# q's low part on 128 partitions, the softmax guard on GpSimd, v without its zero blocks, and new leads for the planner

## The chip, the core and the metric

The kernel runs on one core of a Trainium2 chip. Its engines work side by side, each through its own queue in order: TensorE (PE, with its weight loads shown apart as PEld), VectorE (DVE), ScalarE (ACT), GpSimd (POOL), and SyncE (SP), which issues the DMAs. The metric is the device time of one execution in microseconds; of several runs the median counts.

## The reference, cut to what matters

```python
def reference(q, k, v, f, moe_w_in, moe_w_out, moe2_w_in, moe2_w_out, moe2_alpha):
    # q, k, v: (4, 8, 576, 64) float32, f: (4, 8, 576)
    cum = np.cumsum(np.log(np.clip(f, 0.0001, 1.0)), axis=-1)
    scores = q @ k^T / sqrt(64) + cum[..., :, None] - cum[..., None, :]   # causal: -1e9 above the diagonal
    attn = np.exp(scores - max(scores))
    attn = attn / (np.sum(attn, axis=-1, keepdims=True) + 1e-09)
    x = (attn @ v) as (2304, 512)
    h = x @ moe_w_in;  x = np.maximum(0.01 * h, h) @ moe_w_out            # 512 -> 2048 -> 512
    h = x @ moe2_w_in; g = np.maximum(h, 0) + moe2_alpha * np.minimum(h, 0)
    return g @ moe2_w_out
```

So there are a causal attention with a forgetting decay for 32 heads, and two feed-forward layers (here MoE1 and MoE2) over 2304 tokens.

## The kernel before, in words

**Numbers in two parts.** TensorE multiplies float32r tiles faster than float32 ones, but with fewer bits. So nearly every operand is split in a high part (a cast to float32r) and a low part (the operand minus its high part), and a product becomes three. `cast` (L404 on ScalarE, L406 on VectorE) makes high parts and `sub` (L409) low parts. The expert weights come raw, are taken apart (L487 to L507), split, and partly parked in DRAM scratch (`wscr`), from where they come back as `ws` (L573).

**Stages.** Four batches and two parts of the sequence (queries 0 to 320 and 320 to 576) make 8 groups of 8 heads. The first two groups (some 60 us) use plain float32 and load q, k and v as they are (*native*). The other six groups, 48 heads, use the split form and are laid between MoE1's matmuls (L604 is h, L650 is y), up to about 480 us. MoE1 goes on to 608 us. MoE2 runs from there to the end, with seven products per block (L761) in place of eight, and its second matrix (L830).

**One split head.** SP loads `qk` (L922): 128 partitions, where the upper 64 hold the head's q and k and the lower 64 hold them again. `qk_hi` casts all of it to `k1`. `q_lo` replaces the lower 64 partitions of q's columns with q minus its high part, so that one matmul of 128 rows gives two of the three products. `k_lo` writes k's low part to `k2`. The row of the decay's cumulative sum is broadcast into `cb` by DMA (L929), and GpSimd masks it (`dm`, L1097; for the first heads `cb`, L1104). v arrives in `vr` for two heads at once (L914): the host array has three blocks of 64 columns, the first head's v, zeros and the second head's v; `v_hi` and `v_lo` read the first and the third of them. The scores (L1131) get the decay and the mask on VectorE (L1145), then ScalarE's exp (L1156), which also sums the row into `nm`. A `guard` adds 1e-9 to the sum (L1001) and `recip` inverts it (L1004), both on VectorE, for two rows of blocks at a time. Then the weights are normalised (L1171 on ScalarE, L1173 on VectorE or GpSimd), transposed on TensorE (L1186), split as `pt` (L1202) and multiplied with v (L1034; native L1024). The output is shifted and added into `xr` (L1075, L1078) and split as `xp`.

**What sets the order.** No engine's order is written by hand. `Plan.op` records each operation with its time on each engine that may do it and with a due time; `Plan.run` simulates the engines and lets each take, of the operations that are ready, the one due first. An operation counts as ready when what it reads has ended, plus a latency for the pair of engines (`latency`, L120). Where several engines may do it, the cheapest takes it: VectorE's `shared` operations and GpSimd's exclude each other in the simulation, with `PRICE` on top. The instructions are then issued in the simulated order. The due times come from a row of constants: `PROL`, `PROL0` and `FIRST0` set the first stage, `AHEAD` how early weights are loaded, `W2LEAD`, `W2FROM`, `W2EACH`, `W2STEP` and `W2OUT` when MoE2's weights are made ready, `LEAD1`, `LASTSPAN`, `LASTH` and `ATTN` the pace of the heads, `PACKLEAD` and `DMALAT` the loads.

```python
        return (0 if a == "pe" else 125) if a == b else 260 if b == "pe" else 200 if a == "pe" else 170
```

Of the kernel before, what the change touches and what calls it, by code (L numbers as in the profile page):

```python
# [18 lines left out]

P = 128  # L20
EXCL = 1
WT = {"dve": 1.0, "act": 1.0, "pool": 1.0}
OLD = 0
SUBD = 1
RECIPS = 2
MARGIN = 450
AHEAD = 7600
NRAW = 4
CW = 512
NCV = 3  # L30
NAT = 16
PACKLEAD = 5200
ORDER = (0, 0, 0, 0, 1, 1, 1, 1)
NSTREAM = 18
NSTR = 4
# [8 lines left out]
NGR = 2  # L44
NG = 3
NYSB = 2
W2LEAD = 112200
NEARLY = 4
W2FROM = 2.77
W2EACH = 0.68  # L50
W2LAG = 51000
W2STEP = 5300
W2OUT = 8400
AHEAD2 = 16300
NR = 8
NG2 = 5
# [1 line left out]
NWARM = 5  # L58
PAIRS = (0, 3, 5, 7)
SHIFT = 1  # L60
PROL = 52000
PROL0 = 26000
FIRST0 = 99000
FREE = 8
ATTN = 12800
LASTH = 10600
W1LEAD = 12500
LEAD1 = 24000
LEAD2 = 54900
DMALAT = 2600  # L70
BATCH = 1
LASTSPAN = 1.04
STEP = 4
PRICE = 0.25
MASKED = 2.0**30


# [33 lines left out]
class Plan:  # L111
# [8 lines left out]
    @staticmethod  # L120
    def latency(a, b):

        if "dma" in (a, b):
            return DMALAT * (a == "dma") + 1250 * (b == "dma")
        return (0 if a == "pe" else 125) if a == b else 260 if b == "pe" else 200 if a == "pe" else 170

    def op(self, times, due, fn, r=(), w=(), a=(), after=(), hold=(), shared=False, busy=1.0):

# [148 lines left out]
def t_act(n):  # L277
    return 0.833 * n + 90
# [14 lines left out]
def t_pool1(n):  # L293
    return 0.833 * n + 245
# [19 lines left out]
def tile_forgetting_attention_two_moe(ctx: ExitStack, tc, qk0, qk1, v0, v1, fg, w1, w2, alphaT, out):  # L314
# [126 lines left out]
    rings["g"].ordered = False  # L441
    ring("ysb", NYSB, [P, 2, T])
    ring("qk", 2, [P, 256 + S], pool="att")
    ring("vr", 2, [P, 5, 3, D], pool="att")
    ring("cb", 3, [P, S], pool="att")
    ring("k1", 1, [P, 256 + S], F32R, pool="att")
    ring("k2", 1, [P, S], F32R, pool="att")
# [11 lines left out]
    ring("pt0", 2, [P, 1408], pool="att0")  # L459
    ring("tri", 1, [P, 2 * P], F32R)  # L460

    rate = const.tile([B * H, 2], F32, name="rate")
    warm = const.tile([1, 1], F32, name="warm")
    yd = dram.tile([P, NC, NT], F32, name="yd")
    wscr = dram.tile([NF, 2, P, 2, 512], F32, name="wscr")
    w2in = dram.tile([NP, 4, P, 2, 512], F32, name="w2in")
    cum_d = dram.tile([B * H, 2, S], F32, name="cum_d")

    warm_b, cum_b, yd_b, wscr_b, w2_b, rate_b = (Buf(Ring(1, None)) for _ in range(6))
    for b, ap in ((warm_b, warm), (cum_b, cum_d), (yd_b, yd), (wscr_b, wscr), (w2_b, w2in), (rate_b, rate)):  # L470
        b.ap = ap
    tri_b = new("tri")

# [7 lines left out]
    def assemble(which, f, half, d, after=()):  # L481

        raw, v = new("raw"), new("cv")
        src = (w1, w2)[which].bitcast(I32)[f, :, 2 * CW * half : 2 * CW * (half + 1)]

        def load():
            sp.dma_start(out=raw.ap, in_=src.rearrange("p (n t) -> p n t", t=2))  # L487

        def rebase(e):
            high = f32(raw.ap[:, :, 1])  # L490
            if e == "act":
                act.activation(out=f32(v.ap), in_=high, func=AF.Copy, scale=2.0**-112)
# [12 lines left out]

        def low():
            dve.scalar_tensor_tensor(  # L507
                out=v.ap, in0=raw.ap[:, :, 0], scalar=29, in1=v.ap, op0=ALU.logical_shift_right, op1=ALU.bitwise_or
            )

        on("dma", t_dma(8 * CW * P), EARLY if (which, f) == (0, 0) else d - 5e3, load, w=[raw], after=after)
        plan.op({"act": t_act(CW), "pool": t_pool1(CW)}, d, rebase, r=[raw], w=[v])
        on("dve", t_dve2(CW), d, bits, w=[v], shared=True)
        on("dve", t_dve(CW), d, sign, r=[raw], w=[v], shared=True)
        on("dve", t_dve(CW), d, low, r=[raw], w=[v], shared=True)
        return v
# [353 lines left out]
    def attention_heads(gi, hs, d, span):  # L870
# [29 lines left out]
        for e, h in enumerate(hs):  # L900
# [10 lines left out]
            hi, lo = (0, D) if even else (D, 0)  # L911
            if even:
                vr = x_raw["v"] = new("vr0" if native else "vr")
                on("dma", t_dma(3 * nkt * D * 4 * P), dh - (6e3 if native else 12e3), lambda: sp.dma_start(  # L914
                    out=vr.ap[:, :nkt], in_=g["v"][b, h // 2]), w=[vr])

            apart = not native or gi == 0 and h < 2
            width = n + keys if apart else 2 * (n + keys)
# [12 lines left out]
            def qk_hi(en, k1=k1, qk=qk):  # L931
                cast(en, k1.ap[:, : n + keys], qk.ap[:, : n + keys])

            def q_lo(en, k1=k1, qk=qk):
                sub(en, k1.ap[D:P, :n], qk.ap[D:P, :n], f32(k1.ap[D:P, :n]))

            def k_lo(en, k1=k1, k2=k2, qk=qk):
                sub(en, k2.ap[:, :keys], qk.ap[:, n : n + keys], f32(k1.ap[:, n : n + keys]))

            def v_hi(en, v2=v2, h=h, hi=hi, o2=o2):  # L940
                cast(en, v2.ap[:, o2 : o2 + nkt, hi : hi + D], vr.ap[:, :nkt, h % 2 * 2, :])

            def v_lo(en, v2=v2, h=h, hi=hi, lo=lo, o2=o2):
                sub(en, v2.ap[:, o2 : o2 + nkt, lo : lo + D], vr.ap[:, :nkt, h % 2 * 2, :], f32(v2.ap[:, o2 : o2 + nkt, hi : hi + D]))

            m = full[-1][0] + P
            if apart or e == 0:
# [31 lines left out]
                        lambda: pair.ap[half, both : both + keys], r, keys), r=[(cum_b, g["i"])], w=[(pair, 1 + e)])  # L979
            if not native:  # L980
                plan.op(t_cast(n + keys), dh - 2e3, qk_hi, r=[qk], w=[k1], shared=True)
                plan.op(t_sub(n), dh - 2e3, q_lo, r=[qk], w=[(k1, "q")], shared=True)
                plan.op(t_sub(keys), dh - 2e3, k_lo, r=[qk, (k1, "k")], w=[k2], shared=True)
                plan.op(t_cast(nkt * D), dh + each, v_hi, r=[vr], w=[(v2, (e, "hi"))], shared=True)
                plan.op(t_sub(nkt * D), dh + each, v_lo, r=[vr, (v2, (e, "hi"))], w=[(v2, (e, "lo"))], shared=True)
# [10 lines left out]
        for i, u, t, es, du in todo:  # L996
            if i % RECIPS == 0:
                i1 = min(i + RECIPS, len(todo))

                def guard(i=i, i1=i1):  # L1000
                    dve.tensor_scalar(out=nm.ap[:, 3, i:i1], in0=nm.ap[:, 2, i:i1], scalar1=1e-9, scalar2=None, op0=ALU.add)  # L1001

                def recip(i=i, i1=i1):
                    dve.reciprocal(out=nm.ap[:, 3, i:i1], in_=nm.ap[:, 3, i:i1])  # L1004

                both = [(nm, k) for k in range(i, i1)]
                on("dve", 70, du, guard, w=both)
# [5 lines left out]
    def attention_out(g, t0, h, e, dd, vr, v2, o2, lo, hi, pt, pt_ap, native):  # L1013
# [65 lines left out]
                out=xr.ap[hi : hi + D, :n], in0=po.ap[hi : hi + D, :n], in1=xr.ap[hi : hi + D, :n], op=ALU.add  # L1079
            )  # L1080

        on("act", t_act(n) - 40, dd, shift, r=[po], w=[(xr, h % 2)])
        on("dve", t_dve(n), dd, add, r=[po], w=[(xr, h % 2)])
        if not even:
            split(xr, False)

# [331 lines left out]
```

## Time and profile before

| | us |
|---|---|
| three runs | 992.1, 993.36, 994.47 |
| median | 993.36 |
| profiled execution | 991.83 |
| its span, first to last instruction | 989.7 |

| engine | busy us | share | instructions |
|---|---|---|---|
| TensorE | 976.0 | 99% | 5170 |
| TensorE weight loads | 842.6 | 85% | 5170 |
| VectorE | 746.7 | 75% | 1849 |
| ScalarE | 536.2 | 54% | 1231 |
| GpSimd | 90.1 | 9% | 161 |

Line numbers (L1001) are those of the kernel before. A row names the tiles as out<-in without buffer numbers. Busy time of TensorE counts matmuls with a modelled end, so short gaps vanish in it; the weight loads show them. "<-ACT t L1171" names what ended an idle time: here a tile t written by ScalarE in line 1171. A share over the whole span is a mean over stages that differ.

### The profile page before, as it was taken

How to read it: one execution, taken by the hardware profiler on the slowest of the kernel's cores; microseconds unless marked ns; L12 is line 12 of the kernel's file. 1: busy time of each engine (PE TensorE's matmuls, PEld its weight loads, DVE VectorE, ACT ScalarE, POOL GpSimd, SP SyncE). 2: the span in 40 equal slices, each digit the busy share in tenths (PEclk: the TensorE clock that was granted, in tenths of full speed). 3: DMA queues.
4: the chain of work that ended last, by engine and by line, in shares of the span. 5: the costliest groups of instructions: out<-in, count | busy, mean ns of one | idle time of the engine just before them, and what ended most of it. 6: DMA issues, size and time to landing. Idle time of an engine off the chain costs nothing.

```text
span 989.7 us, 15662 instructions
## 1 busy us (share of the span) xinstructions
PE 976.0 (99%) x5170; PEld 842.6 (85%) x5170; DVE 746.7 (75%) x1849; ACT 536.2 (54%) x1231; POOL 90.1 (9%) x161
## 2 busy tenths in 40 slices
PE   9999999999999999999999999999999999999998
PEld 7777777999888878878878888889889898988987
DVE  7798999887998897986776647856696656856563
ACT  8987887996887777867646435211232112321112
POOL 2101233211211120211000000000000000000000
PEclk9999999999999999999999999999999999999999
DMA  8869887688767789845497765533374333634311
GB/s 285 286 202 320 284 316 229 207 297 285 259 228 267 242 275 320 271 145 174 138 368 253 262 213 173 175 111 118 107 245 129 127 118 107 203 121 144 105 46 64
DMA packets 76128, 203.27 MB, mean 205 GB/s; under 512 B 8112, under 2 KB 23248, under 8 KB 76048
## 3 DMA queue, kind: packets, MB, share of 16 engines
q1 hardware_dynamic: 76048, 202.28, 61.2%
q8 instruction: 41, 0.67, 0.3%
q14 instruction: 39, 0.32, 0.1%
HBM read 168.57 MB, written 33.67 MB: 204 GB/s over the span
## 4 chain that ended last, share of the span: by engine, by line
PE 76%; DVE 10%; issue 6%; DMA 4%; ACT 4%; POOL 1%; POOLq 0%; ACTq 0%; SPq 0%; DVEq 0%
PE bank L830 20%; PE bank L761 18%; PE bank L650 12%; PE bank L604 12%; PE bank L1131 5%; PE bank L1186 3%; PE bank L1034 3%; DMA raw<-w 2%; PE bank L1024 1%; DVE pt L1202 1%; DVE k L409 1%; DVE t L1145 1%; DMA w2in<-wa 1%; DVE cv L507 1%; DVE g L409 1%
## 5 line engine op out<-in xcount | busy, mean ns | idle before, releaser
L830 PE MATMUL bank<-w,g 128*128 128x512 f32 x756 | 196.9, 393 | 0.0
L404 ACT ACTIVATE g<-r 128x384 fp32r<-128x384 f32 x96 | 50.4, 526 | 256.3 <-DVE r L793 232.5
L770 DVE TENSOR_TENSOR r<-bank,r 128x384 f32<-128x384 f32 x168 | 91.0, 555 | 91.1 <-PE bank L761 90.9
L830 PEld LDWEIGHTS bank<-w,g 128*128 128x128 f32 x756 | 140.1, 188 | 21.2
L650 PE MATMUL bank<-g,ws 128*128 128x512 f32 (+1 forms) x540 | 128.0, 374 | 1.3 <-ACT g L404 1.3
L604 PE MATMUL bank<-xp,ws 128*128 128x512 f32 (+1 forms) x540 | 126.3, 372 | 0.0
L650 PEld LDWEIGHTS bank<-g,ws 128*128 128x128 f32 x540 | 92.1, 189 | 18.2 <-ACT g L404 3.7
L604 PEld LDWEIGHTS bank<-xp,ws 128*128 128x128 f32 x540 | 93.3, 189 | 15.2
L650 PE MATMUL bank<-g,w 128*128 128x512 f32 (+1 forms) x420 | 101.4, 375 | 0.1
L604 PE MATMUL bank<-xp,w 128*128 128x512 f32 (+1 forms) x420 | 99.2, 374 | 0.1
L1156 ACT ACTIVATE t<-t,nm 128x128 f32<-128x128 f32 (+4 forms) x144 | 83.9, 586 | 24.6 <-DVE nm L1145 24.2
L604 PEld LDWEIGHTS bank<-xp,w 128*128 128x128 f32 x420 | 72.1, 189 | 12.4 <-ACT t L1171 0.5
L650 PEld LDWEIGHTS bank<-g,w 128*128 128x128 f32 x420 | 71.8, 189 | 12.1 <-ACT g L404 0.7
L1202 DVE TENSOR_TENSOR pt<-bank,pt 128x128 fp32r<-128x128 f32 (+2 forms) x136 | 64.1, 504 | 22.2 <-ACT pt L404 21.7
L1097 POOL TENSOR_SCALAR_AFFINE_SELECT dm<-cb 128x448 f32<-128x448 f32 (+1 forms) x96 | 54.9, 573 | 264.1 <-DVE nm L1145 224.2
L1171 ACT ACTIVATE t<-t,nm 128x128 f32<-128x128 f32 (+4 forms) x112 | 58.8, 564 | 28.7 <-DVE nm L1004 27.5
L409 DVE TENSOR_TENSOR g<-r,g 128x384 fp32r<-128x384 f32 x96 | 53.2, 554 | 25.9 <-ACT g L404 25.9
L404 ACT ACTIVATE pt<-bank 128x512 fp32r<-128x512 f32 (+6 forms) x176 | 67.6, 433 | 4.3 <-PE bank L1186 3.6
L1186 PE MATMUL bank<-tri,t 128*128 128x128 f32 x432 | 65.8, 277 | 1.7 <-DVE t L1173 0.5
L409 DVE TENSOR_TENSOR g<-gr,g 128x512 fp32r<-128x512 f32 x72 | 50.4, 700 | 18.4 <-ACT g L404 18.3
L1186 PEld LDWEIGHTS bank<-tri,t 128*128 128x128 f32 x432 | 49.3, 141 | 15.0 <-ACT t L1171 5.3
L1034 PEld LDWEIGHTS bank<-pt,v 128*128 128x128 f32 x416 | 55.8, 189 | 5.9 <-ACT pt L404 1.9
(136 smaller groups left out, 1687.0 us busy)
## 6 DMA issues: line engine op xcount, KB each, us to landing
ws<-wscr SPq DMA_DIRECT2D x72, 512.0 KB, 4.9
raw<-w SPq DMA_DIRECT2D x64, 512.0 KB, 5.8
wa<-w2in SPq DMA_DIRECT2D x33, 512.0 KB, 3.5
ws<-w2in SPq DMA_DIRECT2D x33, 512.0 KB, 3.5
qk<-qk SPq DMA_DIRECT2D x32, 416.0 KB, 4.7
wscr<-ws SPq DMA_DIRECT2D x18, 512.0 KB, 5.6
cb<-cum_d SPq DMA_DIRECT2D x32, 288.0 KB, 4.4
vr<-v SPq DMA_DIRECT2D x16, 480.0 KB, 5.1
```

The lines of the kernel that those rows point to most:

```text
L404: act.activation(out=out, in_=in_, func=AF.Copy)
L409: (dve if e == "dve" else gps).tensor_tensor(out=out, in0=in0, in1=in1, op=ALU.subtract)
L604: pe.matmul(h()[:, i] if single else h(), lhsT=w.ap[:, a, c * P : (c + 1) * P], rhs=xs[0].ap[:, s, c] if single else xp[:, x0 : x0 + 2, s, c],
L650: pe.matmul(out(c), lhsT=w.ap[:, a, col : col + P], rhs=g.ap[:, s, at : at + n], start=f == 0 and (a, s) == (0, 0) and (c % 2 == 0 or not ...
L761: pe.matmul(b.ap[:, :N2], lhsT=t.ap[:, a, o + c * P : o + (c + 1) * P], rhs=view(k)[:, s, c], start=c == 0 and i == 0, stop=c == 1 and i == 2,
L770: on("dve", t_dve(N2), d + k * step - URGENT, lambda: dve.tensor_tensor(out=out.ap, in0=b.ap[:, :N2], in1=x.ap, op=ALU.add), r=[b] if x is ...
L830: pe.matmul(acc[j * (N2 // P) + t].ap, lhsT=g.ap[:, s, t * P : (t + 1) * P], rhs=w.ap[:, a], start=p == 0 and i == j and (a, s) == (0, 0), ...
L1034: pe.matmul(po.ap[:, q:n], lhsT=v2.ap[:, o2 + j, :], rhs=pt_ap(s, e, j, j + 1, q, n), start=s == 0 and j == 0, stop=s == 1 and j == nkt - 1,)
L1156: act.activation(out=t.ap[:, :nk], in_=t.ap[:, :nk], func=AF.Exp, scale=-1.0, bias=nm.ap[:, last, u : u + 1], accum_out=nm.ap[:, 2, u : u ...
L1171: act.activation(out=t.ap[:, :nk], in_=t.ap[:, :nk], func=AF.Copy, scale=nm.ap[:, 3, u : u + 1])
L1186: pe.transpose(tp.ap[:, (j - j0) * P : (j - j0 + 1) * P], t.ap[:, k0 : k0 + P], f32(tri_b.ap[:, :P]))
L1202: dve.tensor_tensor(out=lo, in0=src, in1=f32(hi), op=ALU.subtract)
```

## The change

Four things change. `q_lo` is no longer a subtraction on 64 partitions by VectorE or GpSimd, but one scalar_tensor_tensor on all 128 by VectorE alone: high part times a column `lower` plus q, where the column is 0 for the upper 64 partitions and −1 for the lower (a new tile `rates` holds it beside the old `rate`). The guard's addition goes to GpSimd, the reciprocal stays on VectorE. Split heads load only the two blocks of v that are read, so that each partition's row becomes pieces of 256 bytes; native heads load as before. And the planner's latencies, times and due times are set anew; latencies have names now. Lines shift by 5 (around L490 to L930) and then by 7.

```diff
+TOSAME = 125
+TOPE = 315
+FROMPE = 200
+CROSS = 200
-AHEAD = 7600
+AHEAD = 5100
-PACKLEAD = 5200
+PACKLEAD = 6100
...
-PROL = 52000
-PROL0 = 26000
-FIRST0 = 99000
+PROL = 53600
+PROL0 = 24200
+FIRST0 = 94700
...
-DMALAT = 2600
+DMALAT = 3200
...
-        return (0 if a == "pe" else 125) if a == b else 260 if b == "pe" else 200 if a == "pe" else 170
+        return (0 if a == "pe" else TOSAME) if a == b else TOPE if b == "pe" else FROMPE if a == "pe" else CROSS
...
-    ring("vr", 2, [P, 5, 3, D], pool="att")
+    ring("vr", 2, [P, 5, 2, D], pool="att")
...
-    rate = const.tile([B * H, 2], F32, name="rate")
+    rates = const.tile([P, 3], F32, name="rates")
+    rate, lower = rates[: B * H, :2], rates[:, 2:]
...
-        plan.op({"act": t_act(CW), "pool": t_pool1(CW)}, d, rebase, r=[raw], w=[v])
+        plan.op({"act": t_act(CW) + 50, "pool": t_pool1(CW)}, d, rebase, r=[raw], w=[v])
...
-                on("dma", t_dma(3 * nkt * D * 4 * P), dh - (6e3 if native else 12e3), lambda: sp.dma_start(
-                    out=vr.ap[:, :nkt], in_=g["v"][b, h // 2]), w=[vr])
+                on("dma", t_dma((2 + native) * nkt * D * 4 * P), dh - (6e3 if native else 12e3), lambda: sp.dma_start(
+                    out=vr.ap[:, :nkt], in_=g["v"][b, h // 2] if native else g["v"][b, h // 2][:, :, ::2]), w=[vr])
...
-            def q_lo(en, k1=k1, qk=qk):
-                sub(en, k1.ap[D:P, :n], qk.ap[D:P, :n], f32(k1.ap[D:P, :n]))
+            def q_lo(k1=k1, qk=qk):
+                dve.scalar_tensor_tensor(
+                    out=k1.ap[:, :n], in0=f32(k1.ap[:, :n]), scalar=lower, in1=qk.ap[:, :n], op0=ALU.mult, op1=ALU.add
+                )
...
-                plan.op(t_sub(n), dh - 2e3, q_lo, r=[qk], w=[(k1, "q")], shared=True)
+                on("dve", t_dve(n), dh - 2e3, q_lo, r=[qk, lower_b], w=[(k1, "q")], shared=True)
...
-                    dve.tensor_scalar(out=nm.ap[:, 3, i:i1], in0=nm.ap[:, 2, i:i1], scalar1=1e-9, scalar2=None, op0=ALU.add)
+                    gps.tensor_scalar(out=nm.ap[:, 3, i:i1], in0=nm.ap[:, 2, i:i1], scalar1=1e-9, scalar2=None, op0=ALU.add)
...
-                on("dve", 70, du, guard, w=both)
+                on("pool", 180, du, guard, w=both)
...
-        on("act", t_act(n) - 40, dd, shift, r=[po], w=[(xr, h % 2)])
-        on("dve", t_dve(n), dd, add, r=[po], w=[(xr, h % 2)])
+        on("act", t_act(n) + 90, dd, shift, r=[po], w=[(xr, h % 2)])
+        on("dve", t_dve(n) + 100, dd, add, r=[po], w=[(xr, h % 2)])
...
+    for i in range(2):
+        on("pool", 100, -9.4e3, lambda i=i: gps.memset(lower[i * D : i * D + D], -1.0 * i), a=[(lower_b, i)])
```

The rest of the constants: W2LEAD 112200 to 114600, W2FROM 2.77 to 2.753, W2EACH 0.68 to 0.762, W2STEP 5300 to 4900, W2OUT 8400 to 9300, ATTN 12800 to 12200, LASTH 10600 to 13600, LEAD1 24000 to 24800, LASTSPAN 1.04 to 1.083, PRICE 0.25 to 0.141.

Three places show how the order moves. The first is VectorE's queue at 608 us, where MoE1 ends. `bx`, `xp`, `xt` and `yraw` belong to MoE2's input, `w` is one of its weights, `ws` a weight from scratch. Before:

```order
L409 TENSOR_TENSOR ws_7168<-cv_6369,ws_7168 128x256
L406 CAST w_7184<-cv_7112 128x512
L409 TENSOR_TENSOR w_7184<-cv_7112,w_7184 128x512
L409 TENSOR_TENSOR bx_6254<-yraw_7153,bx_6254 128x384
L409 TENSOR_TENSOR xp<-yraw_7153,xp 128x384
L409 TENSOR_TENSOR bx_6307<-yraw_7153,bx_6307 128x384
```

Now:

```order
L413 TENSOR_TENSOR ws_7169<-cv_6381,ws_7169 128x256
L413 TENSOR_TENSOR bx_6292<-yraw_7123,bx_6292 128x384
L413 TENSOR_TENSOR xp<-yraw_7123,xp 128x384
L413 TENSOR_TENSOR bx_6347<-yraw_7123,bx_6347 128x384
...
L413 TENSOR_TENSOR bx_6336<-xt_7200,bx_6336 128x384
L413 TENSOR_TENSOR xp<-yraw_7123,xp 128x384 x2
L413 TENSOR_TENSOR w_7224<-cv_7141,w_7224 128x512
```

The cast of `w` has left VectorE's queue for ScalarE's, and its low part has moved behind all of the splits of MoE2's first input.

The second is GpSimd's queue in the first stage: `cb` masks (L1104, now L1111), rebased weights `cv` (L494, now L499), and guards (`nm`, L1008). Before:

```order
L1104 TENSOR_TENSOR cb_0_145<-cb_0_145,tri_115 64x64 x2
L1104 TENSOR_TENSOR cb_1_163<-cb_1_163,tri_115 64x64 x2
L494 TENSOR_SCALAR cv_241<-raw_182 128x512
L494 TENSOR_SCALAR cv_267<-raw_202 128x512
L1104 TENSOR_TENSOR cb_2_221<-cb_2_221,tri_115 64x64 x2
```

Now:

```order
L1111 TENSOR_TENSOR cb_0_150<-cb_0_150,tri_118 64x64 x2
L1008 TENSOR_SCALAR nm_0_138<-nm_0_138 128x2
L1111 TENSOR_TENSOR cb_1_175<-cb_1_175,tri_118 64x64 x2
L1008 TENSOR_SCALAR nm_0_138<-nm_0_138 128x2
L1008 TENSOR_SCALAR nm_0_138<-nm_0_138 128x1
L499 TENSOR_SCALAR cv_242<-raw_180 128x512
L1008 TENSOR_SCALAR nm_1_191<-nm_1_191 128x2 x2
L1008 TENSOR_SCALAR nm_1_191<-nm_1_191 128x1
L1111 TENSOR_TENSOR cb_2_244<-cb_2_244,tri_118 64x64 x2
L1008 TENSOR_SCALAR nm_2_248<-nm_2_248 128x2
```

The guards stand between the masks, so a guard is begun only when the mask ahead of it is done, and that mask when its `cb` has been loaded.

The third is VectorE's queue in the split attention: q's low part (`k_0`, 64x256 before, 128x256 now), k's (128x576), the guard and the reciprocal of `nm`, and the decay (L1145, now L1152, whose second row reads the row maximum out). Before:

```order
L409 TENSOR_TENSOR k_0_2863<-qk_2743,k_0_2863 64x256
L409 TENSOR_TENSOR k_0_2887<-qk_2743,k_0_2863 128x576
L1001 TENSOR_SCALAR nm_2782<-nm_2782 128x2
L1004 RECIPROCAL nm_2782<-nm_2782 128x2
L1078 TENSOR_TENSOR xr_2874<-bank_71,xr_2874 64x256
L1173 TENSOR_SCALAR t_2788<-t_2788,nm_2782 128x576
```

Now:

```order
L1152 ISA t_2822,nm_2823<-bank_72,dm_2772 128x448
L1152 ISA nm_2823 128x1
L1011 RECIPROCAL nm_2740<-nm_2740 128x2
L413 TENSOR_TENSOR xp<-xr_2776,xp 128x64
L1180 TENSOR_SCALAR t_2739<-t_2739,nm_2740 128x448
...
L940 SCALAR_TENSOR_TENSOR k_0_2844<-k_0_2844,rates,qk_2745 128x256
L1152 ISA t_2829,nm_2823<-bank_74,dm_2814,nm_2823 128x192
L1152 ISA nm_2823 128x1
L413 TENSOR_TENSOR k_0_2874<-qk_2745,k_0_2844 128x576
```

The guard has left VectorE's queue; the reciprocal stands alone and waits for GpSimd, with the next decay ahead of it, and q's low part is a different instruction on twice the partitions.

## Rows read from the trace of the kernel before

**Rows 1.** The page, busy time (share of the span) and instructions by engine.

```profile
PE 976.0 (99%) x5170; PEld 842.6 (85%) x5170; DVE 746.7 (75%) x1849; ACT 536.2 (54%) x1231; POOL 90.1 (9%) x161
```

**Rows 2.** Busy us by stage: stretch, length, engines (instructions), clock, DMA share, GB/s.

```profile
0.00:60.00 60.00, 57.76 (x314) 45.42 (x315) 44.85 (x188) 54.53 (x190) 10.05 (x31) 1.00 0.79 261
60.00:200.00 140.00, 136.54 (x756) 114.52 (x755) 127.98 (x347) 111.62 (x283) 35.25 (x60) 1.00 0.81 268
200.00:510.00 310.00, 306.69 (x1799) 263.16 (x1798) 264.79 (x699) 233.15 (x500) 44.77 (x70) 1.00 0.73 248
```

**Rows 3.** Chain that ended last: start, us, engine, operation, matmuls (MoE1).

```profile
524.19 2.72 PE bank L650 x12
```

**Rows 4.** Timeline at 608 us: start, us, engine, operation [idle before, releaser].

```profile
608.54 0.43 DVE L406 CAST w<-cv 128x512 fp32r<-128x512 f32 x1 [1.84 <-PE bank L650]
609.01 0.69 DVE L409 TENSOR_TENSOR w<-cv,w 128x512 fp32r<-128x512 f32 x1
...
605.62 2.88 PE L650 MATMUL bank<-g,w 128*128 128x512 f32 x12
...
610.22 0.97 PE L761 MATMUL bank<-bx,wa 128*128 128x384 f32 x4 [0.85 <-DVE bx L409]
```

**Rows 5.** TensorE weight-load waits (us, times, longest): 200 to 510, then 60 to 200.

```profile
PEld bank L1131 <- issue: 2.4, 5, 0.7
...
PEld bank L650 <- ACT ysb L404: 0.2, 1, 0.2
...
PEld bank L1186 <- ACT t L1171: 2.6, 8, 0.7
...
PEld bank L1186 <- DVE xr L1078: 0.2, 1, 0.2
```

**Rows 6.** Guards by shape: busy us, mean ns, idle before; then normalisation (page).

```profile
L1001 DVE TENSOR_SCALAR nm<-nm 128x2 f32<-128x2 f32 x64 | 11.7, 182 | 3.6 <-ACT t L1156 3.2
L1171 ACT ACTIVATE t<-t,nm 128x128 f32<-128x128 f32 (+4 forms) x112 | 58.8, 564 | 28.7 <-DVE nm L1004 27.5
```

**Rows 7.** VectorE busy in the guards of line 1001, by stage.

```profile
0.00:60.00 60.00, 4.14 (x24) 1.00 0.79 261
60.00:200.00 140.00, 4.14 (x21) 1.00 0.81 268
200.00:510.00 310.00, 5.58 (x35) 1.00 0.73 248
```

**Rows 8.** GpSimd by shape: busy us, mean ns, idle before and what ended it.

```profile
L409 POOL TENSOR_TENSOR k<-qk,k 64x320 fp32r<-64x320 f32 x4 | 5.2, 1291 | 15.7 <-ACT k L404 11.6 <-issue 4.1
L1173 POOL TENSOR_SCALAR t<-t,nm 128x128 f32<-128x128 f32 x1 | 0.5, 544 | 0.4 <-DVE v L406 0.4
L1409 POOL MEMSET const-float32-0.0<- 128x1 f32 x1 | 0.1, 103 | 0.2 <-issue 0.2
L1104 POOL TENSOR_TENSOR cb<-cb,tri 64x64 f32<-64x64 f32 x32 | 12.8, 402 | 52.1 <-DMA cb<-cum_d 38.5 <-ACT cb L404 8.5 <-DVE t L1173 2.8
```

**Rows 9.** VectorE splits by shape: busy us, mean ns, idle before.

```profile
L409 DVE TENSOR_TENSOR k<-qk,k 64x256 fp32r<-64x256 f32 x32 | 13.6, 426 | 1.6 <-ACT k L404 0.8
L409 DVE TENSOR_TENSOR k<-qk,k 64x320 fp32r<-64x320 f32 x12 | 6.3, 522 | 0.6 <-ACT k L404 0.2
L409 DVE TENSOR_TENSOR k<-qk,k 128x320 fp32r<-128x320 f32 x14 | 7.2, 516 | 0.1
L793 DVE SCALAR_TENSOR_TENSOR r<-r,gr 128x384 f32<-128x384 f32 x96 | 53.5, 557 | 2.2
```

**Rows 10.** DMA packets, MB, share: 192:450, 979:989; landings, lines 929, 914.

```profile
q1 hardware_dynamic: 22688, 66.53, 76.4%
...
q1 hardware_dynamic: 1728, 1.57, 47.1%
...
DMA to landing us min/median/max: 3.0/5.0/8.0
...
DMA to landing us min/median/max: 2.9/5.2/7.2
```

More of the change, by code (lines that the diff above doesn't have):

```diff
@@ L46 @@
 NYSB = 2
-W2LEAD = 112200
+W2LEAD = 114600
 NEARLY = 4
-W2FROM = 2.77
-W2EACH = 0.68
+W2FROM = 2.753
+W2EACH = 0.762
 W2LAG = 51000
-W2STEP = 5300
-W2OUT = 8400
+W2STEP = 4900
+W2OUT = 9300
 AHEAD2 = 16300
@@ L60 @@
 SHIFT = 1
-PROL = 52000
-PROL0 = 26000
-FIRST0 = 99000
+PROL = 53600
+PROL0 = 24200
+FIRST0 = 94700
 FREE = 8
-ATTN = 12800
-LASTH = 10600
+ATTN = 12200
+LASTH = 13600
 W1LEAD = 12500
-LEAD1 = 24000
+LEAD1 = 24800
 LEAD2 = 54900
-DMALAT = 2600
+DMALAT = 3200
 BATCH = 1
-LASTSPAN = 1.04
+LASTSPAN = 1.083
 STEP = 4
-PRICE = 0.25
+PRICE = 0.141
 MASKED = 2.0**30
@@ L467, in tile_forgetting_attention_two_moe @@
     cum_d = dram.tile([B * H, 2, S], F32, name="cum_d")
-    warm_b, cum_b, yd_b, wscr_b, w2_b, rate_b = (Buf(Ring(1, None)) for _ in range(6))
-    for b, ap in ((warm_b, warm), (cum_b, cum_d), (yd_b, yd), (wscr_b, wscr), (w2_b, w2in), (rate_b, rate)):
+    warm_b, cum_b, yd_b, wscr_b, w2_b, rate_b, lower_b = (Buf(Ring(1, None)) for _ in range(7))
+    for b, ap in ((warm_b, warm), (cum_b, cum_d), (yd_b, yd), (wscr_b, wscr), (w2_b, w2in), (rate_b, rate), (lower_b, lower)):
         b.ap = ap
@@ L940, in v_hi @@
             def v_hi(en, v2=v2, h=h, hi=hi, o2=o2):
-                cast(en, v2.ap[:, o2 : o2 + nkt, hi : hi + D], vr.ap[:, :nkt, h % 2 * 2, :])
+                cast(en, v2.ap[:, o2 : o2 + nkt, hi : hi + D], vr.ap[:, :nkt, h % 2, :])
             def v_lo(en, v2=v2, h=h, hi=hi, lo=lo, o2=o2):
-                sub(en, v2.ap[:, o2 : o2 + nkt, lo : lo + D], vr.ap[:, :nkt, h % 2 * 2, :], f32(v2.ap[:, o2 : o2 + nkt, hi : hi + D]))
+                sub(en, v2.ap[:, o2 : o2 + nkt, lo : lo + D], vr.ap[:, :nkt, h % 2, :], f32(v2.ap[:, o2 : o2 + nkt, hi : hi + D]))
             m = full[-1][0] + P
```

## The prediction

> **What bounds the kernel now.** I read the page's busy shares first, then the busy time of each engine by stage, then TensorE's waits in each stage, and then the queues of the engines that these waits name. The page gives TensorE 976.0 of 989.7 us, at a granted clock of 1.00 (the 2.4 GHz level) in every stage [rows 1, 2]. VectorE and ScalarE have room in the mean, but not everywhere: ScalarE is busy 54.53 of the first 60 us (91%), and VectorE 127.98 of the next 140 (91%) [rows 2]. Since the change takes no matmul away, it can only alter what TensorE idles. By stage that is 60.00 − 57.76 = 2.24 us (0 to 60), 3.46 (60 to 200) and 3.31 (200 to 510) [rows 2]; behind 510 us the longest is 0.85 at 608 [rows 4].
>
> These numbers are too small, because the profile models the end of a matmul. A dozen 512-column matmuls take 2.72 us on the chain of waits (0.227 us each), while the last twelve before a gap are shown as 2.88 [rows 3, 4]. So each gap hides some 0.16 us. The weight loads show the gaps unhidden: 45 waits in 200 to 510 (16 rows, 17.0 us of idle weight loading, part of it beside running matmuls) and 21 in 60 to 200 (11 rows, 8.9 us); the largest row of the second has eight of at most 0.7 us [rows 5]. What can be had is therefore 3.31 + 45 × 0.16 = 10.5 us in the first of these stretches and 3.46 + 21 × 0.16 = 6.8 in the second. These are many short waits for ScalarE and VectorE (normalisation t, pt low parts, g), which is what a planner's leads decide.
>
> **The change, part by part.** All terms stand against the profiled execution, 991.83 us (span 989.7 and 2.1 around it).
>
> *New leads, at 608 us: −1.0.* Where the first expert layer ends, VectorE idles 1.84 us for a weight buffer that TensorE's last y product still holds; behind that stand a cast (0.43) and a low part (0.69) of w, and only then comes bx, for which TensorE waits [rows 4]. TensorE idles 0.85 us there, 1.0 with the hidden part. In the new order the cast is gone to ScalarE, the low part stands behind all bx and xp splits, and so nothing that waits for that buffer is ahead of bx. w is first read only behind nine products of six 384-column matmuls, some 9 us later, so nothing new is late. The bounds are 0 and −1.0.
>
> *New leads, 200 to 510 us: −3.0.* The planner now assumes 315 ns instead of 260 from another engine to TensorE and 200 instead of 170 between the others. I followed each matmul in both orders back to the VectorE or ScalarE instruction that it waits for and summed the matmuls in between (0.227 us for 512 columns). Places with less than 1 us in between fall from 29 to 9; those with less than 1.2 us of VectorE's and ScalarE's together from 82 to 46. By the first count 10.5 × 20/29 = 7.2 us would go, by the second 10.5 × 36/82 = 4.6. But such a count leaves out why an instruction started late, and some of the named waits come from issue and DMA, which no lead alters [rows 5]. I take −3.0, nearer to the second, and keep 0 and −7.2.
>
> *Guard on GpSimd.* There are 80 guards, 182 ns each where they are 128x2 [rows 6]; by stage they take 4.14, 4.14 and 5.58 us, 13.9 off VectorE [rows 7]. Where VectorE is 91% busy this is worth something; elsewhere it is not the bound. On GpSimd the trace has nothing of 128x2: a fill of 128x1 took 103 ns, a 128x128 TENSOR_SCALAR 544 [rows 8], and I take 250. GpSimd is busy 90.1 of 989.7 us [rows 1], so room is there. The price is one more hand-over in the chain exp, guard, reciprocal, normalisation, on which ScalarE already idled 27.5 us in 28 places [rows 6]. Queued behind the reciprocal are VectorE's next decay, splits and xr adds, and TensorE for them.
>
> For 60 to 200 us I take −2.0: half of the 4.14 us that leave the full VectorE. The bounds are −4.1 and, if the longer chain eats it, 0. For 0 to 60 us I take +1.0: ScalarE is full there, so VectorE's relief gains nothing, and 24 reciprocals wait one hand-over longer. The bounds are 0 and, at 0.4 us for each (250 ns and a hand-over, less the 182), 24 × 0.4 = +9.6, though the order starts the guards further ahead: the matmuls between exp and transpose rise from 2.2 to 3.0 us.
>
> *q's low part: 0.* 44 VectorE and 4 GpSimd instructions on 64 partitions become 48 on 128. A column count sets the time: 256 columns on 64 partitions took 426 ns, 320 columns 522 on 64 and 516 on 128; and a SCALAR_TENSOR_TENSOR of 384 columns took 557, no more than that line gives [rows 9]. So four more of 0.43 to 0.52 us, 1.9 us over 400, where VectorE has 45 us free between 200 and 510 [rows 2]. If none of that hides it is +1.9. The four on GpSimd had cost 1291 ns each [rows 8].
>
> *v without the zero block: +0.3.* Only the 24 loads of the split heads change (8 of 128x6x64, 16 of 128x10x64). A row of 3840 bytes becomes ten pieces of 256: 1280 pieces, 80 on each of 16 engines. From 192 to 450 us the engines move 66.53 MB in 76.4% of 258 us, that is 66.53/(16 × 197) = 21 bytes per ns; before, a load held each engine 8 × 3840/21 ns = 1.46 us. At the same rate 80 pieces take 0.98 us. The worst row is the output store, 1728 packets in 47.1% of 10 us: 16 × 4.71/1728 = 44 ns each, and 80 of these are 3.5 us [rows 10]. So between −0.5 and +2.0 us for each of 24 loads, on engines with a share of 0.73 to 0.81 [rows 2], and the loads land 5.2 us after issue, in the median, where the planner issues them 12 us ahead. That lead hides the difference, so I take +0.3; the ends are −0.3 and, with one load late in full, +2.0 in all.
>
> The Trainium skill's "DMA: Bandwidth & Descriptors", table of specifications, says that below 512 bytes a transfer loses line rate because it is read, modified and written. By that rule 80 pieces cost as much as 80 of 512 bytes, an estimate of 1.95 us, and the new load is the dearer one although it moves a third less. No row here prices a piece under 512 bytes alone; by the rule the sum stays within its ends.
>
> *Tail: 0.* The last 236 rows of TensorE's order and the queues beside them are unchanged. Loads of the weight scratch are issued later (AHEAD 5100 for 7600), but their least distance from issue to use stays 5.1 to 5.5 us, the thinnest cover of all; if it breaks, TensorE waits for ws.
>
> The sum: −1.0 − 3.0 − 2.0 + 1.0 + 0.3 = −4.7, 987.1 for the profiled execution. The median of the runs before is 993.36, 1.53 above the profiled one, so 988.7.
>
> **The rivals.** A change within 0.2%, 2.0 us, is about what a measurement of this kernel can't tell from none.
>
> First, *more goes than I take*: 200 to 510 loses 7.2 as the first count says, 60 to 200 loses 2.0 to 4.1, and 0 to 60 costs nothing: −1.0 − 7.2 − 2.0 + 0.3 = −9.9, 983.5. For it: waits of 0.2 to 0.7 us, which a few hundred ns of lead do end. Against it: from 60 to 200 TensorE's largest sum of waits belongs to ScalarE's normalisation, not to VectorE [rows 5].
>
> Second, *the waits only change their name*: the leads move the same work among the same full engines, 200 to 510 and 60 to 200 give nothing, and what is left is −1.0 + 1.0 + 0.3, thus 993.7. For it: both engines are 85% and 75% busy there [rows 2], and 16 different waits share those 45 places. It also stands for the case that the change does not relieve VectorE, because guard time comes back as waiting for the guard.
>
> Third, the slower side: *a guard behind a mask that waits for its DMA*. In the new order GpSimd's guards stand behind cb masks, whose loads land 5.0 us after issue in the median and 8.0 at most [rows 10]; masks waited 38.5 us for them in all [rows 8], at no cost then because nothing else queued there. Now a late mask holds the guard, the guard the reciprocal, and that VectorE's whole queue. In eight places before 200 us the matmuls between that load's issue and the reciprocal are only 5.3 to 6.2 us. A landing midway, at 6.5 us, with 0.3 for the mask, would be 0.6 to 1.5 us late; with 0.8 at each, these stages cost 6.4 instead of −1.0: −1.0 − 3.0 + 0.3 + 6.4 = +2.7, 996.1. The rival decides from (993.36 + 2.0 − 988.7 − 1.0) / 8 = 0.7 us for each place. Against it: the median landing is just in time, and the planner sets each load 6.5 us ahead of its head.
>
> The Trainium skill's "SBUF — State Buffer", on SBUF's two separate sides, has a rule that strengthens this rival: VectorE and GpSimd share a port pair as an exclusive lock, so a VectorE instruction with two SBUF inputs blocks a GpSimd one that reads SBUF. No row here shows the lock apart (a mask's mean of 402 ns [rows 8] may hold some of it); by it each of the eight guards could start up to 0.69 us later, the longest split shown [rows 4], which would make 1001.6 of the 996.1. The price above does not use it.
>
> **How the numbers follow.** The forecast gets 0.42 (own range 985.5 to 991.3), the larger gain 0.16, the unchanged time 0.22, the slower one 0.20. That makes faster 0.58, same 0.22, slower 0.20. The range of 983 to 996 leaves out about half of the first and of the third rival.
>
> **What would show it.** In the profile after, TensorE's wait for bx at the layers' boundary is gone; the waits in 200 to 510 us sum to well under 17 us; VectorE loses 14 us of guards, and its row of reciprocals shows little idle time for GpSimd; q's low part takes 0.43 us for 256 columns; v lands within 7 us. The forecast is wrong if VectorE waits several us for nm from GpSimd before 200 us, if TensorE waits for a weight load ws, or if as many short waits for t and pt stand there as before.

## The result, and the profile after

The changed kernel takes 977.56 us in the median of four runs (977.16 to 977.92), the kernel before 993.53. The ratio is 0.984 with a 95% interval of 0.9823 to 0.9857: 16.0 us less. The direction was forecast, the size was not: 988.7 us were predicted, and 977.56 lies below the range's low end of 983.0. The profiled execution took 977.92, its span 976.1. Of the edits kernel below, one execution (1603.77 us, at a granted clock of 0.556) stands apart from the other three and is left out of its time.

The page of the changed kernel, and its stages as in [rows 1, 2]:

```profile
PE 967.6 (99%) x5170; PEld 844.6 (87%) x5170; DVE 746.7 (76%) x1793; ACT 520.6 (53%) x1205; POOL 123.7 (13%) x245
```

```profile
0.00:60.00 60.00, 57.71 (x306) 44.73 (x307) 45.76 (x171) 52.40 (x179) 20.02 (x58) 1.00 0.83 270
60.00:200.00 140.00, 138.93 (x803) 120.00 (x802) 128.49 (x344) 114.89 (x300) 39.67 (x83) 1.00 0.82 266
200.00:510.00 310.00, 308.72 (x1814) 270.34 (x1813) 270.08 (x678) 220.45 (x473) 64.03 (x104) 1.00 0.76 246
```

VectorE is busy for 746.7 us in both kernels. The guards are gone, but q's low part takes longer per instruction, and the planner has moved work of ScalarE to VectorE (38 normalisations in place of 31, 28 casts of g and v in place of 17), so "relief" below means a shorter queue in a given order and not less busy time in the whole.

TensorE's idle time fell from 3.46 to 1.07 us between 60 and 200 us and from 3.31 to 1.28 between 200 and 510. Since short gaps vanish in these numbers, the waits of the weight loads say more. From 200 to 510 us (first and last of 15 rows):

```profile
PEld bank L655 <- DVE g L410: 1.3, 2, 1.1
...
PEld bank L1041 <- DVE pt L1209: 0.2, 1, 0.2
```

Those rows sum to 6.0 us in 21 waits, where before it was 17.0 in 45 [rows 5]; from 60 to 200 us it is 3.5 in 9 for 8.9 in 21. At the boundary of the two layers (timeline as in [rows 4]) nothing stands between the products any more, and bx follows VectorE's last ws split without idle time:

```profile
594.39 0.42 DVE L413 TENSOR_TENSOR ws<-cv,ws 128x256 fp32r<-128x256 f32 x1
594.72 0.55 DVE L413 TENSOR_TENSOR bx<-yraw,bx 128x384 fp32r<-128x384 f32 x1
...
593.80 2.20 PE L655 MATMUL bank<-g,w 128*128 128x512 f32 x9
595.84 1.20 PE L766 MATMUL bank<-bx,wa 128*128 128x384 f32 x6
```

The guard on GpSimd, and VectorE's waits for it (min/median/max in ns; then us in total, times, longest, from 0 to 510 us):

```profile
L1008 POOL TENSOR_SCALAR nm<-nm x80: 212/362/1828, 10.9 to 473.1; 128x2 f32<-128x2 f32 x64, 128x1 f32<-128x1 f32 x16
```

```profile
DVE nm L1011 <- POOL nm L1008: 2.0, 3, 1.0
```

A guard takes longer than the 250 ns that I took, yet VectorE waited for it only three times. Nor did the end of the chain wait longer: ScalarE's normalisation idled 16.0 us for the reciprocal, after 27.5 [rows 6]:

```profile
L1178 ACT ACTIVATE t<-t,nm 128x128 f32<-128x128 f32 (+4 forms) x105 | 54.3, 548 | 16.3 <-DVE nm L1011 16.0
```

The loads of v land after 4.3 us in the median and 7.6 at most, for 5.2 and 7.2 before [rows 10]. The 7.6 is a native head's, which the change leaves alone; the loads of the split heads land within 6.6.

### The profile page after: what moved, and what is told of

The parts are those of the page before. It is cut to its first block, busy times and chain, and to the rows that moved or that the text cites. A ratio compares the mean times of both kernels' runs of the same rounds, so it can differ in the third digit from the quotient of the medians.

```text
span 976.1 us, 15709 instructions
## 1 busy us (share of the span) xinstructions
PE 967.6 (99%) x5170; PEld 844.6 (87%) x5170; DVE 746.7 (76%) x1793; ACT 520.6 (53%) x1205; POOL 123.7 (13%) x245
## 4 chain that ended last, share of the span: by engine, by line
PE 87%; DVE 7%; ACT 2%; DMA 2%; issue 1%; SPq 0%; ACTq 0%; POOL 0%; DVEq 0%
PE bank L835 20%; PE bank L766 18%; PE bank L609 17%; PE bank L655 17%; PE bank L1138 5%; PE bank L1193 4%; PE bank L1041 4%; DMA raw<-w 2%; PE bank L1031 1%; DVE cv L507 1%; ACT t L1163 1%; DVE cv L512 1%; DVE pt L1209 1%; DVE g L413 1%; DVE t L1152 1%
## 5 line engine op out<-in xcount | busy, mean ns | idle before, releaser
L1163 ACT ACTIVATE t<-t,nm 128x128 f32<-128x128 f32 (+4 forms) x144 | 83.5, 582 | 16.3 <-DVE nm L1152 15.7
L1104 POOL TENSOR_SCALAR_AFFINE_SELECT dm<-cb 128x448 f32<-128x448 f32 (+1 forms) x96 | 52.3, 546 | 205.9 <-DVE nm L1152 147.7
L408 ACT ACTIVATE pt<-bank 128x128 fp32r<-128x128 f32 (+6 forms) x174 | 67.6, 430 | 7.8 <-PE bank L1193 7.1
L1178 ACT ACTIVATE t<-t,nm 128x128 f32<-128x128 f32 (+4 forms) x105 | 54.3, 548 | 16.3 <-DVE nm L1011 16.0
L618 ACT ACTIVATE gr<-bank 128x512 f32<-128x512 f32 x72 | 42.6, 593 | 35.1 <-PE bank L609 34.4
```

Source lines behind the costliest of these rows:

```text
L408: act.activation(out=out, in_=in_, func=AF.Copy)
L1163: act.activation(out=t.ap[:, :nk], in_=t.ap[:, :nk], func=AF.Exp, scale=-1.0, bias=nm.ap[:, last, u : u + 1], accum_out=nm.ap[:, 2, u : u ...
L1178: act.activation(out=t.ap[:, :nk], in_=t.ap[:, :nk], func=AF.Copy, scale=nm.ap[:, 3, u : u + 1])
```

## The experiments

Two kinds of kernel take part. Some let the planner lay the order anew. Others keep an order, word for word on every engine, and exchange an instruction in place: the planner's entry stays as it was and only what it emits differs.

**The leads alone, the edits alone.** The first has the code before with the new numbers, the second the changed code with the old ones.

```diff
 # leads, from the kernel before (and so on for every number of the change)
-AHEAD = 7600
+AHEAD = 5100
-        return (0 if a == "pe" else 125) if a == b else 260 if b == "pe" else 200 if a == "pe" else 170
+        return (0 if a == "pe" else 125) if a == b else 315 if b == "pe" else 200 if a == "pe" else 200
 # edits, from the changed kernel (likewise)
-AHEAD = 5100
+AHEAD = 7600
-TOPE = 315
+TOPE = 260
```

> The kernel before with the planner's new latencies, times and due times, and none of the three edits (guard, q's low part and the v load as before). Theory A, the leads give the gain: 978 to 984 us. Theory B, the edits give it (VectorE rid of 13.9 us of guards): 988 to 994. Theory C, both are needed because the leads were set for the edited kernel: 984 to 988, with waits left between 60 and 200 us.

> The changed kernel with the planner's old latencies, times and due times; the three edits stay. Theory A (leads): 988 to 995 us. Theory B (edits): 977 to 983. Theory C (both): 985 to 990.

Measured: leads 988.19 us (ratio 0.996, 0.9945 to 0.9975), edits 997.78 (1.0061, 1.0044 to 1.0078). Neither makes the gain, and the edits alone are slower than before. Each run lost its time in one place. In the leads kernel (stages, then ScalarE, then the weight loads):

```profile
30.00:40.00 10.00, 7.22 (x31) 5.07 (x29) 6.75 (x28) 7.01 (x24) 0.97 (x2) 0.83 0.92 330
```

```profile
31.57 0.66 ACT L492 ACTIVATE cv<-raw 128x512 f32<-128x512 f32 x1 [2.94 <-DMA raw<-w]
```

```profile
34.41 0.30 PEld L1131 LDWEIGHTS bank<-qk 128*128 128x128 f32 x2 [3.34 <-DVE nm L1145]
```

ScalarE waits 2.94 us for a raw weight, VectorE's unpacking of that weight stands ahead of a decay, and TensorE waits 3.34 us for the decay. The granted clock of these ten microseconds is 0.83 in the mean, so for a part of them, with TensorE idle before it, the lower level (1.2 GHz) was granted. In the edits kernel VectorE's queue is full from 120 us on (19.47 of 20), and in the next stretch TensorE runs dry, at a clock of 0.74:

```profile
120.00:140.00 20.00, 20.00 (x109) 16.75 (x107) 19.47 (x51) 17.43 (x46) 7.60 (x12) 1.00 0.78 267
140.00:160.00 20.00, 13.24 (x52) 9.80 (x51) 16.92 (x41) 13.19 (x33) 4.34 (x7) 0.74 0.66 222
```

In its three executions the mean granted clock is 0.994 to 0.995. By an estimate, 0.005 of 997.78, some 5 us of its time are the clock's, and it takes 5.7 longer than the kernel before on that chip (992.11).

So a lost kernel here is not one with many small waits more, but one with a place where a queue runs over, and where the clock then falls. My count of places with less than 1 us of matmuls between giver and taker (29 before, 9 after) does not show it: by it the edits kernel has 53 of them from 200 to 520 us (no view shows this count), and its weight loads wait 11.0 us from 200 to 510, less than the 17.0 before.

**The numbers of the first stage, and 5 ns more or less.**

```diff
 # leads_old_start, from leads (and so for PROL0 and FIRST0)
-PROL = 53600
+PROL = 52000
 # lead_310, and lead_320 likewise, from the changed kernel
-TOPE = 315
+TOPE = 310
```

> The kernel before with the new leads, but the first stage's three numbers (PROL, PROL0, FIRST0) as they were. Theory D: the new leads are worth about 10 us on the kernel before too, and the run with all of them loses 5 us of that in one stall at 31 us, where VectorE stands behind a weight whose load lands late and TensorE's clock then falls; without that stall 981 to 985. Theory C, the leads fit only the edited kernel and gain little without the edits: 987 to 990, with no stall over 1.5 us before 60 us.

> The changed kernel with 310 ns in place of 315 for the hand-over to TensorE, everything else equal; the planner then lays all instructions anew. Places with under 1 us of matmuls between giver and taker from 200 to 520 us rise from 9 to 17. Theory E, the time depends on how the order happens to fall more than on the size of any lead: 980 to 990. Theory A: 977 to 979, 5 ns of lead are nothing.

> The changed kernel with 320 ns in place of 315 for the hand-over to TensorE; the planner lays everything anew. Theory E (how the order happens to fall): 980 to 990 us, with at least one place before 500 us where TensorE loses over 2 us that the changed kernel does not lose. If 310 ns was too small a lead and not another draw: 976 to 979.

Measured: 997.08 us (1.0045, 1.0031 to 1.0059), 982.45 (0.9896, 0.9875 to 0.9918) and 979.67 (0.9878, 0.9863 to 0.9893). The old start does not take the stall away: the weight loads wait 2.29 us up to 34 us, and four times 1.2 to 1.4 us between 158 and 166 us, where the clock falls again (0.66 in the mean from 160 to 170). Theory D thus failed in this form. A lead 5 ns larger or smaller costs 2 to 5 us, though the order is laid by the same rules; at 320 the interval still overlaps the changed kernel's (0.9844 to 0.9873 in a second measurement below). At 310 a part of the loss is the clock: it is 0.69 in the mean from 160 to 170 us, and the four executions go from 980.8 us at a mean clock of 1.000 to 984.37 at 0.997. The 320 kernel has one wait of 1.6 us at 258 us and otherwise looks like the changed one; its time lies just under what theory E gave, above what the other gave, and the place with over 2 us that theory E asked for is not there. So larger leads are not shown to be better ones. That the set on hand is a good draw together with these edits fits these times; it is not shown.

**One edit undone at a time, in the new order.**

```diff
 # guard_dve
-gps.tensor_scalar(out=nm.ap[:, 3, i:i1], ...
+dve.tensor_scalar(out=nm.ap[:, 3, i:i1], ...
 # guard_mix
+(dve if native else gps).tensor_scalar(out=nm.ap[:, 3, i:i1], ...
 # v_zero_block
-ring("vr", 2, [P, 5, 2, D], pool="att")
+ring("vr", 2, [P, 5, 3, D], pool="att")
 # q_half, q_half_again
-dve.scalar_tensor_tensor(out=k1.ap[:, :n], ..., scalar=lower, ...)
+sub("dve", k1.ap[D:P, :n], qk.ap[D:P, :n], f32(k1.ap[D:P, :n]))
 # q_stt_half
+dve.scalar_tensor_tensor(out=k1.ap[D:P, :n], ..., scalar=lower[D:P], ...)
```

> The changed kernel with the guard's addition on VectorE at the very place in the program where GpSimd's stands; every other instruction keeps its order. Theory A (leads): 977 to 981 us, at most the 4.1 us of guards between 60 and 200 us come back. Theory B (edits, the guard above all): 984 to 992, 13.9 us of VectorE on the way to TensorE. A third possibility, that the hand-over by GpSimd costs more than it saves: 973 to 977.

> The changed kernel with v loaded with its zero block again (one piece of 3840 bytes per partition in place of ten of 256); the order of all engines is unchanged. Theories A and B: 976.5 to 978.5 us, the loads are hidden. If the shorter load (a third less bytes) is part of the gain: 980 or more. If the short pieces hold the DMA engines: 975 or less.

Measured: guard 982.44 us (0.9902, 0.9888 to 0.9917), v 977.55 (0.9851, 0.9834 to 0.9867). The guard on GpSimd is worth 4.9 us in a fixed order, v nothing. With the guard on VectorE the waits of the weight loads are 6.0 us from 60 to 200 and 9.9 from 200 to 510, for 3.5 and 6.0.

> The changed kernel with the guard on VectorE for the native heads (first 60 us) and on GpSimd for the split ones; the order is unchanged. Guards on GpSimd cost the first stage some 0.5 to 0.8 us by the two profiles and gain 5.4 behind it: 976.5 to 977.5 us. If the gain of the guard on GpSimd lies in the first stage after all: 979 to 982.

Measured 978.13 us (0.9852, 0.9832 to 0.9872), 0.6 above what I expected and not to be told from the changed kernel: the guard's gain lies behind the first stage, and in the first it costs nothing that shows in the time.

> The changed kernel with q's low part as a subtraction on 64 partitions again, on VectorE at the same place; the order of all engines is unchanged. If instructions are priced by columns alone: 976.5 to 978.5 us. If the operation on 128 partitions with a per-partition column is dearer on VectorE (its 256 columns took 484 ns in the median where the old one took 426): 975 to 976.5. If it is part of the gain: over 979.

> The changed kernel itself, for a comparison on one chip with the three others of this call: 976.5 to 978.5 us.

> The changed kernel with q's low part on 64 partitions again, once more and in more rounds. If the 2 to 3 us of its first run are the operation's: 979 to 981, 1.5 us or more above the changed kernel of this call. If they were the run's or the chip's: within 1 us of it.

Measured: 980.35 us (0.9874, 0.9855 to 0.9893) at first, then 980.93 (0.9893, 0.9879 to 0.9907) beside 977.13 (0.9859, 0.9844 to 0.9873) for the changed kernel itself. So q's low part on 128 partitions is worth 3.8 us, though each instruction lasts longer. The timeline shows why (start, us, engine, operation). The changed kernel, VectorE at 122 us:

```profile
122.13 0.68 DVE L413 TENSOR_TENSOR g<-gr,g 128x512 fp32r<-128x512 f32 x1
122.73 0.54 DVE L940 SCALAR_TENSOR_TENSOR k<-k,rates,qk 128x320 fp32r<-128x320 f32 x1
123.19 0.69 DVE L413 TENSOR_TENSOR ws<-cv,ws 128x512 fp32r<-128x512 f32 x1
```

The same three instructions with the subtraction on 64 partitions:

```profile
123.63 0.69 DVE L413 TENSOR_TENSOR g<-gr,g 128x512 fp32r<-128x512 f32 x1
124.35 0.49 DVE L413 TENSOR_TENSOR k<-qk,k 64x320 fp32r<-64x320 f32 x1
124.87 0.69 DVE L413 TENSOR_TENSOR ws<-cv,ws 128x512 fp32r<-128x512 f32 x1
```

Above, each starts some 80 ns before its predecessor's recorded end; below, 30 ns behind it. From the start of g to that of ws it is 1.06 us above and 1.24 below, with the shorter instruction in the middle. Over all 48, 34 on 128 partitions overlap their predecessor and 46 are overlapped by their successor; on 64 it is 4 and 0.

> The changed kernel with the same scalar_tensor_tensor for q's low part, but on the lower 64 partitions alone; order unchanged. In the traces an instruction on 64 partitions did not start before its predecessor ended (31 ns behind it), one on 128 started some 80 ns before. If the partitions do that: 979.5 to 981.5 us, as with the subtraction on 64. If the kind of operation does it: 976.5 to 978.5.

Measured 981.94 us (0.9902, 0.9887 to 0.9917). It is the partitions, not the kind of operation:

```profile
122.48 0.68 DVE L413 TENSOR_TENSOR g<-gr,g 128x512 fp32r<-128x512 f32 x1
123.19 0.55 DVE L940 SCALAR_TENSOR_TENSOR k<-k,rates,qk 64x320 fp32r<-64x320 f32 x1
123.78 0.69 DVE L413 TENSOR_TENSOR ws<-cv,ws 128x512 fp32r<-128x512 f32 x1
```

Here it is 1.30 us from g to ws, and again 4 of 48 overlap before and none behind.

**The relief in the old order, the new order without it.**

```diff
 # no_guard_new_order, no_guard_old_order
-gps.tensor_scalar(...)  /  dve.tensor_scalar(...)
-dve.reciprocal(out=nm.ap[:, 3, i:i1], in_=nm.ap[:, 3, i:i1])
+dve.reciprocal(out=nm.ap[:, 3, i:i1], in_=nm.ap[:, 2, i:i1])
 # old_order_relieved: no_guard_old_order, and in q_lo
+if en == "dve": dve.scalar_tensor_tensor(out=k1.ap[:, :n], ..., scalar=lower, ...)
 # order_alone: guard_dve, v_zero_block and q_half together
```

> The changed kernel without the guard: the 1e-9 is left out (a row's sum is at least 1, since its largest score gives exp(0), so float32 does not change), the reciprocal reads the sum itself, the order stays. If the hand-over through GpSimd still costs something: 975 to 977. If GpSimd hides it wholly: 977 to 978.5. If a reciprocal that no longer waits runs VectorE into other waits: over 979.

> The kernel before in its own order, without the guard (the 1e-9 left out, the reciprocal reads the sum), so that VectorE has the same 13.9 us less as in the changed kernel. Theory F, VectorE's relief is worth about 5 us in any order: 986 to 989. Theory C, the relief pays only in the new order: 990.5 to 993. The prediction's own price, 2 us: 990 to 991.

Measured: 978.04 us (0.9863, 0.9848 to 0.9878) and 988.58 (0.9964, 0.9952 to 0.9975). GpSimd hides the guard wholly, and taking it off VectorE is worth 3.5 us in the old order too, as theory F had it. By the intervals that is not to be told from the 4.9 us in the new order.

> The changed kernel's order with all three edits undone in place: guard and q's 64-partition low part on VectorE, v with its zero block. If the parts add up (4.9 us for the guard, 3.4 for q, none for v): 985 to 987 us, and the order alone is worth 5 to 7. If they overlap (each removes the same waits): 982 to 985. If the order lives on the relief: 988 to 993.

> The kernel before in its own order, without the guard (1e-9 left out) and with q's low part on 128 partitions where VectorE makes it (44 of 48). If the relief pays the same in any order: 984 to 987 us (992.1 less 3.5 less some 3.4). If q's part pays only in the new order: 987.5 to 990.

Measured: 984.86 us (0.9932, 0.9917 to 0.9947) and 984.71 (0.9931, 0.9914 to 0.9947), against 991.79 for the kernel before on that chip. Order and relief are worth 7 us each, whether the other is there or not: 0.9932 × 0.9931 = 0.9863, where the changed kernel has 0.9859. Which of the many numbers makes the new order better, no run takes apart. The waits of the weight loads (us) say the same:

| kernel | 60 to 200 | 200 to 510 | 510 to 660 |
|---|---|---|---|
| before | 8.9 | 17.0 | 1.6 |
| new order, no relief | 7.1 | 11.8 | 0 |
| old order, relieved | 5.2 | 12.0 | 1.6 |
| changed | 3.5 | 6.0 | 0 |

**The output's adds on 128 partitions.** The adds of the split heads' output (L1085) run on 64 partitions as well.

```diff
+if not even:
+    return dve.scalar_tensor_tensor(
+        out=xr.ap[:, :n], in0=po.ap[:, :n], scalar=below, in1=xr.ap[:, :n], op0=ALU.mult, op1=ALU.add)
```

> The changed kernel with the output's add (line 1085) of every second split head (24 of 48) as a scalar_tensor_tensor on all 128 partitions, with a column that is 0 above and 1 below, in place of an add on the lower 64; order unchanged. If it is the 64 partitions that cost VectorE some 0.1 us per instruction, and 40% of VectorE's relief reaches TensorE as for the guard and q: 24 x 0.1 x 0.4, thus 1 us less, 976 to 977. If the source in PSUM keeps these instructions apart anyway: 977 to 978.5.

Measured 975.43 us (0.9834, 0.9821 to 0.9847), 1.7 less than the changed kernel's 977.13 and below the range expected. With the 0.18 us by which the timelines above differ (1.24 less 1.06) in place of 0.1, the same sum gives 1.7, an estimate after the fact. It is the lowest median of all, but not settled: its interval overlaps that of 977.13, and the changed kernel's first ratio, 0.984, is the same.

## Why the prediction was right or wrong

**608 us, −1.0: right.** TensorE's wait for bx is gone, and with it 1.6 us of weight-load waits, in every kernel with the new numbers. Of weight-load waits from 510 to 660 us these kernels have none, but for 0.3 at 310 ns and 0.7 in the first run of q_half, neither of them for bx.

**The leads, −3.0 from 200 to 510 us: too small for what the order gave, the mechanism not borne out.** The order alone gave 6.9 us (0.9932) for the 4.0 that I gave the leads at 608 and behind 200 us; the rest is between 60 and 200 us, where the waits fell from 8.9 to 7.1 without relief, and in 200 to 510 us, where 17.0 became 11.8. That larger leads do this is not shown: no run changes the two latencies alone by their full step (260 to 315, 170 to 200). The same numbers without the edits gave 3.9 us (there the waits fell to 4.7 and 13.6 behind 60 us, and rose from 7.9 to 13.5 before it), and 5 ns more or less gave 2 to 5 back.

**The guard, −2.0 + 1.0: the step that failed.** I gave VectorE's relief a price only where its stage is 91% busy ("elsewhere it is not the bound") and half of the guards' time there. In a fixed order it is 4.9 us. Between 60 and 200 us the price was about right: with the guard back on VectorE the waits are 6.0 us there, for 3.5. The failure is 200 to 510 us, which I put at nothing and where 3.9 us of waits come back (9.9 for 6.0). VectorE is 85% busy there [rows 2], but that mean hides slices like this one from the trace of the kernel before, VectorE third after the length:

```profile
260.00:270.00 10.00, 9.82 (x55) 7.87 (x55) 9.86 (x28) 7.67 (x17) 1.55 (x2) 1.00 0.45 144
```

Of 31 slices of 10 us between 200 and 510 us, 12 have VectorE at 95% or more, of the 45 from 60 us on 18. I added up the weight loads' waits (gaps over 150 ns) from 60 to 510 us by slice. With the guard on VectorE the 20 full slices hold 12.0 us and the others 3.7; in the changed kernel, in the same order, its 20 full ones hold 7.8 and the others 1.6. So two thirds of what the guard's move takes away goes in slices where VectorE is full. Fullness alone does not make the waits: in the kernel before, the 27 slices with room hold 15.3 us of them and the 18 full ones 10.8.

**q's low part, 0: failed too.** I priced it by the instruction's duration (426 and 516 ns [rows 9]), by which the new one is no cheaper; measured it lasts 482 ns for 256 columns. It is 3.8 us cheaper because of the gaps beside it: the run with the same operation on the lower 64 partitions gives the gain back. The prediction's "a column count sets the time" holds for how long an instruction lasts, not for when the next one starts.

**The sum.** Predicted: order −4.0, relief −1.0, v +0.3. Measured: order −6.9, relief −7.1 (in the old order), v 0. By these parts the miss is 9.3 us, and two thirds of it is the relief.

**0 to 60 us, +1.0: the sign right by luck.** Its waits rose from 7.9 to 9.3 us, but nothing of that can be put to the guard: with the guard on VectorE there they are 8.8 (guard_dve) and 9.3 (guard_mix), and a second profile of the changed kernel has 8.9. The bound of +9.6 was too high by its own terms as well: 250 ns and the planner's 200 for a hand-over, less 182, are 0.27 us and not 0.4, thus +6.4.

**v, +0.3: hidden, as said.** In the same order the loads with the zero block landed after 4.4 us in the median, without it after 4.3. The trace of the changed kernel also prices the short pieces, for which the prediction had no row: its 26,624 packets of 256 bytes took 18 ns each in the median, and in v_zero_block one of 3840 took 149 (190 in the mean). So 80 short ones are 1.44 us, and 8 long ones 1.19 or, by the mean, 1.52. The Trainium skill's "DMA: Bandwidth & Descriptors", table of specifications, would make the short pieces the dearer load; here the two are about even, and 1.44 is less than the 1.95 us estimated from it. A load's lead would have covered either.

**The rivals.** The larger gain had the right direction, but it was 6 us short and its source (lead counts) is not borne out. The guard behind a late mask did not come about: VectorE waited 2.0 us in three places. That waits change their name was wrong for this order. The leads without the edits come nearer to it: the waits went from later stretches to the first.

## What to carry to other kernels

Price an instruction by the distance from its predecessor's start to its successor's, not by its duration. Where an order comes out of a planner, exchange one instruction in place and keep the order: only so is a part's price told from the luck of the draw. Here the same code took 977.56 and 997.78 us with two sets of the planner's numbers, and 5 ns in one of them moved the time by 2 to 5 us. An engine at 85% in the mean can be full in 12 slices of 31; look at slices before calling relief worthless.

## What the runs showed of the hardware

When two VectorE instructions on all 128 partitions follow one another, the second mostly starts some 80 ns before the recorded end of the first (1206 of 1467 such pairs less than 150 ns apart in the changed kernel). q's low part on partitions 64 to 127 does not overlap so: its predecessor ended 31 ns earlier, and its successor began some 14 ns after it (medians over 48). It is not the number of partitions: of the 48 adds of line 1085 in the changed kernel, 19 of the 24 on partitions 0 to 63 overlap their predecessor and 17 their successor, and none of the 24 on 64 to 127 does either (the two kinds alternate).

Nor is it the lower half as such. The 4 of 48 low parts that did overlap all stood right behind an add on the same lower half (in q_half, q_half_again and q_stt_half alike). In q_stt_half two adds of L1085, the second of them on the lower half, end at 102.70 us, and the low part starts before that:

```profile
101.70 1.00 DVE L1085 TENSOR_TENSOR xr<-bank,xr 64x320 f32<-64x320 f32 x2
102.63 0.55 DVE L940 SCALAR_TENSOR_TENSOR k<-k,rates,qk 64x320 fp32r<-64x320 f32 x1
```

So the overlap went with neighbours that begin at the same partition. The other way round, a low part ahead of an add on the lower half, the add began 31 ns behind it in both cases; that add also reads another memory (PSUM). Why, the runs do not show.

A GpSimd TENSOR_SCALAR of 128x2 took 212 to 1828 ns with a median of 362; its longest cost nothing here.
